# 32-query groups on 64-row array tiles for the attention of three batches out of four, 64-query groups kept for the first

## The chip, the cores and the metric

One core of a Trainium2 chip runs the whole program; everything is fp32. The metric is the device time of one execution in microseconds (us), lower is better. A verdict "faster" or "slower" needs 2%. One execution of the kernel before took 1261.8 us; it lies over 1.5% above the fastest, so it counts as slow and is left out of every ratio.

## The reference

Four batches, eight heads, 768 positions, head width 64. Attention looks at a local window and at 24 block summaries; the result feeds a Fourier mixing layer and a two-layer dense network.

```python
k_sum = k.reshape(B, H, nb, 32, D).max(axis=3)          # 24 blocks of 32
v_sum = v.reshape(B, H, nb, 32, D).mean(axis=3)
scores_l = scale * q @ k.T          where |i - j| < 16, else -1e9
scores_s = scale * q @ k_sum.T + log(32)
x = softmax([scores_l, scores_s]) @ [v, v_sum]          # heads side by side: 768 x 512
u = x + real(fft(fft(x, axis=1), axis=2))
un = (u - mean(u)) / sqrt(var(u) + 1e-6)
out = u + relu(un @ w1) @ w2                            # 512 -> 2048 -> 512
```

## The kernel before: the parts that matter

Heads go in pairs; a batch has four pairs. A *wide* pair is cut into 12 groups of 64 queries, each with a window of 96 keys. The 24 block summaries are rows 96 to 127 of the same score tile, so that one exponential and one mask serve both.

```python
def prepare(b, g):                    # "turning" q and k of a pair, on TensorE
    for src, dst in ((kn, kt), (qn, qt)):
        for j0, j1 in ((0, 2), (2, 3)):
            ps = abank(...)
            # ... 24 matmuls against ident for q and k together, 64-column tiles
            nc.scalar.copy(out=dst[:, 2*P*j0:2*P*j1], in_=ps)      # 4 copies in all, 128 partitions

def scores(b, g):
    for half in range(2):
        for n in range(n0, n1):                                    # 6 groups
            for e in range(2):                                     # 2 heads: two row halves
                nc.tensor.matmul(ps[e][0:96, n - n0, :], kt[rows, 64*n:64*n + 96], qt[rows, 64*n:64*n + 64])
        for e in range(2):
            nc.tensor.matmul(ps[e][96:128], km[rows, :], qt[rows, ...])         # block summaries, 384 columns
        for e in range(2):
            nc.scalar.activation(out=p[:, e, n0:n1], in_=ps[e], func=AF.Exp, scale=SC)
            tt(p[:, e, n0:n1], p[:, e, n0:n1], near[:, n0:n1], ALU.mult)
```

After attention a batch passes through `gen_post`: a Fourier step (`y`), mixing (`mx`: six tiles, each followed on VectorE by the sum with x and the statistics), normalisation and transposes (`unt`), then the dense layers `h` and `o`, which take most of the time.

```python
for t in range(NST):                                  # 6 tiles of 128 positions
    if t % 2: nc.scalar.activation(out=un[:, t, :], in_=x[:, t, :], func=AF.Identity, bias=..., scale=...)
    else:     nc.vector.tensor_scalar(out=un[:, t, :], in0=x[:, t, :], ...)
    for d in range(NDT): nc.tensor.transpose(ps[:, d // 2, d % 2, :], un[:, t, P*d:P*(d+1)], ident)
    (nc.vector.tensor_copy if t % 2 else nc.scalar.copy)(out=u[...], in_=ps)
    yield
```

The attention of batch b + 1 is woven into the post part of batch b, one of its steps after every four of post. Batch 0's attention comes first and alone; batch 1's lies beside batch 0's post part and the conversion of the weights.

```python
for b in range(B):
    attn = gen_attention(b + 1) if b + 1 < B else iter(())
    if b == 0:
        drive((gen_fourier(0), 4, 600), (first(weights, 16), 3, 0), (first(attn, 5), 1, 0))
        drive((gen_channel(0), 4, 0), (weights, 12, 0), (attn, 1, 0))
    else:
        drive((gen_post(b), 4, 0), (attn, 1, 0))
```

I call the time from the first Fourier matmul of batch n to that of batch n + 1 "stage n", and split it at the first mixing matmul (mx), the first transpose of the normalised rows (unt) and the first dense matmul (h).

## Time and profile before

| | us |
|---|---|
| runs before the prediction | 891.82, 892.23 (and the slow 1261.8) |
| stage 0 (batch 1's attention, weight conversion) | 82.2 to 298.8: 216.6 |
| stage 1 (batch 2's attention) | 298.8 to 504.5: 205.7 |
| stage 2 (batch 3's attention) | 504.5 to 707.8: 203.3 |
| stage 3 (no attention) | 707.8 to 881.8: 174.0 |

The windows of the kernel before, cut at the first three of these stages. Columns: window and length, then busy time (with instructions) of PE, PEld, DVE, ACT and POOL, then granted clock, DMA share, GB/s.

```profile
82.20:298.80 216.60, 208.29 (x1209) 152.32 (x1210) 186.03 (x405) 81.74 (x159) 33.45 (x22) 0.99 0.58 183
298.80:504.50 205.70, 205.70 (x1317) 153.45 (x1316) 100.35 (x226) 42.80 (x90) 1.07 (x2) 1.00 0.37 116
504.50:707.80 203.30, 203.30 (x1272) 150.76 (x1270) 100.00 (x229) 41.08 (x86) 0.00 (x0) 1.00 0.30 100
```

TensorE is busy for all of stages 1 and 2.

### The profile page before, as it was taken

The page shows a single profiled execution, that of the slowest core. Times are in us where ns is not written, and L with a number is a line of the kernel's source. Part 1 is how long each engine was busy: PE and PEld are TensorE (multiplying, and loading weights), DVE is VectorE, ACT ScalarE, POOL GpSimd, SP SyncE. Part 2 cuts the span into 40 slices and gives each one's busy share as a digit, 9 for nine tenths or more (in the row PEclk, how much of TensorE's full clock was granted, in tenths as well). Part 3 has the DMA queues.
Part 4 walks back from the last instruction along what each step waited for, and adds up shares of the span by engine and source line. Part 5 has one row for each costly group of instructions (what it writes and reads, how often), then busy time and mean ns, then how long its engine had stood idle before and what let it go on. Part 6 is the DMA issues. An engine that isn't in the chain of part 4 may idle for free.

```text
span 887.9 us, 12940 instructions
## 1 busy us (share of the span) xinstructions
PE 850.9 (96%) x5282; PEld 630.0 (71%) x5282; DVE 505.3 (57%) x1118; ACT 223.5 (25%) x449; POOL 56.0 (6%) x46
## 2 busy tenths in 40 slices
PE   7977999999989999999999999999999988999997
PEld 5755765688558786678758887668757875687586
DVE  1488999976898266353239248254328455442352
ACT  2543365621630224311120034311020022101200
POOL 2404004002050000000000000000000000000000
PEclk9996999999999999999999999999999999999999
DMA  9996776943761463231621372320421171305001
GB/s 207 245 289 169 216 208 215 268 158 110 256 230 42 173 210 105 82 105 36 215 74 60 112 246 60 93 83 1 161 102 59 56 282 44 120 4 189 18 25 50
DMA packets 90020, 119.41 MB, mean 134 GB/s; under 512 B 40448, under 2 KB 73440, under 8 KB 89952
## 3 DMA queue, kind: packets, MB, share of 16 engines
q1 hardware_dynamic: 89408, 117.99, 43.4%
q8 instruction: 43, 0.70, 0.3%
q10 hardware_dynamic: 544, 0.51, 0.2%
q14 instruction: 25, 0.20, 0.1%
HBM read 97.52 MB, written 20.97 MB: 133 GB/s over the span
## 4 chain that ended last, share of the span: by engine, by line
PE 86%; DVE 9%; ACT 2%; DMA 1%; issue 1%; POOL 1%; SPq 0%
PE ox L939 19%; PE hx L892 17%; PE oz L939 9%; PE hz L892 8%; PE sc L606 5%; PE oy L939 4%; PE qk L587 4%; PE hy L892 4%; PE sc L610 3%; PE y L810 3%; PE av L629 3%; PE mx L831 2%; PE mx L833 2%; DVE w L525 2%; DVE fold L525 1%; PE unt L869 1%
## 5 line engine op out<-in xcount | busy, mean ns | idle before, releaser
L892 PE MATMUL hx<-u,w 128*128 128x384 f32 x512 | 184.6, 491 | 4.7 <-ACT h L907 3.1
L892 PEld LDWEIGHTS hx<-u,w 128*128 128x128 f32 x512 | 94.9, 190 | 72.0 <-ACT h L907 5.5
L892 PE MATMUL hz<-u,w 128*128 128x384 f32 x256 | 93.7, 486 | 0.0
L939 PE MATMUL ox<-w,s 128*128 128x256 f32 x384 | 91.8, 382 | 1.7 <-DVE x L525 1.7
L939 PE MATMUL oz<-w,s 128*128 128x256 f32 x384 | 91.6, 379 | 0.0
L939 PE MATMUL ox<-w,h 128*128 128x256 f32 x384 | 89.1, 380 | 0.0
L525 DVE TENSOR_TENSOR x<-ox,x 128x256 f32<-128x256 f32 x96 | 40.5, 423 | 74.4 <-PE ox L939 74.2
L939 PEld LDWEIGHTS ox<-w,s 128*128 128x128 f32 x384 | 71.9, 190 | 14.3 <-DVE x L525 3.0
L939 PEld LDWEIGHTS ox<-w,h 128*128 128x128 f32 x384 | 72.8, 190 | 11.6 <-issue 0.2
L939 PEld LDWEIGHTS oz<-w,s 128*128 128x128 f32 x384 | 72.9, 190 | 10.0 <-issue 0.2
L892 PEld LDWEIGHTS hz<-u,w 128*128 128x128 f32 x256 | 48.6, 190 | 34.0 <-DVE u L525 0.3
L525 DVE TENSOR_TENSOR p<-p,near 128x384 f32<-128x384 f32 x64 | 36.0, 601 | 41.8 <-ACT p L612 41.8
L606 PEld LDWEIGHTS sc<-qt,kt 64*96 64x96 f32 x768 | 41.2, 173 | 20.8 <-issue 12.9
L525 DVE TENSOR_TENSOR h<-hy,h 128x384 f32<-128x384 f32 x32 | 17.8, 556 | 60.5 <-PE hy L892 60.5
L612 ACT ACTIVATE p<-sc 128x384 f32<-128x384 f32 x64 | 28.1, 488 | 88.7 <-PE sc L610 88.7
L606 PE MATMUL sc<-qt,kt 64*96 64x64 f32 x768 | 46.2, 262 | 3.2 <-ACT qt L589 2.7
L892 PE MATMUL hy<-u,w 128*128 128x384 f32 x128 | 46.5, 486 | 0.0
L525 DVE TENSOR_TENSOR h<-hx,h 128x384 f32<-128x384 f32 x32 | 17.8, 556 | 49.5 <-PE hx L892 49.5
L939 PE MATMUL oy<-w,h 128*128 128x256 f32 x192 | 45.6, 380 | 0.0
L816 ACT COPY big<-y 128x192 f32<-128x192 f32 x32 | 10.5, 333 | 133.5 <-PE y L810 133.4
L810 PE MATMUL y<-fs,fold 128*128 128x193 f32 x192 | 37.1, 343 | 6.5 <-DVE fold L795 6.5
L525 DVE TENSOR_TENSOR x<-oz,x 128x256 f32<-128x256 f32 x48 | 20.3, 423 | 36.8 <-PE oz L939 36.8
(92 smaller groups left out, 1111.7 us busy)
## 6 DMA issues: line engine op xcount, KB each, us to landing
w<-dw SPq DMA_DIRECT2D x48, 896.0 KB, 5.1
raw<-in_moe_w_ch_dram SPq DMA_DIRECT2D x32, 512.0 KB, 4.8
dw<-w SPq DMA_DIRECT2D x16, 896.0 KB, 5.9
vw<-in_v_dram SPq DMA_DIRECT2D x30, 288.0 KB, 4.8
kn<-in_k_dram SPq DMA_DIRECT2D x16, 384.0 KB, 4.5
qn<-in_q_dram SPq DMA_DIRECT2D x16, 384.0 KB, 6.0
vb<-in_v_dram SPq DMA_DIRECT2D x16, 384.0 KB, 4.7
out_dram<-x SPq DMA_DIRECT2D x24, 256.0 KB, 2.0
```

Of the source, the lines that this page charges most:

```text
L525: nc.vector.tensor_tensor(out=out, in0=in0, in1=in1, op=op)
L587: nc.tensor.matmul(ps[D * e:D * (e + 1), 2 * P * (j - j0) + s:2 * P * (j - j0 + 1):2], src[:, e, j, D * s:D * (s + 1)], ident, start=True, ...
L606: nc.tensor.matmul(ps[e][0:WK, n - n0, :], kt[rows, QB * n:QB * n + WK], qt[rows, QB * n:QB * (n + 1)], start=True, stop=True)
L610: nc.tensor.matmul(ps[e][WK:P], km[rows, :], qt[rows, QB * n0:QB * n1], start=True, stop=True)
L612: nc.scalar.activation(out=p[:, e, n0:n1], in_=ps[e], func=AF.Exp, scale=SC)
L629: nc.tensor.matmul(av[e][QB * (n % 2):QB * (n % 2 + 1), n // 2, :], p[:, e, n, :], vw[:, e, n, :], start=True, stop=True)
L810: nc.tensor.matmul(y, fgs[par][:, st, P * g:P * (g + 1)], fs[par][:, g % 2, st, :], start=(st == 0), stop=(st == HT - 1))
L816: nc.scalar.copy(out=ty[:, g, par:S2:2], in_=y[:, 0:F2])
L831: nc.tensor.matmul(ps[:, par, :], yt[:, half, 2 * par, cols], fd[:, 3 * par, :], start=True, stop=False)
L833: nc.tensor.matmul(ps[:, par, :], yt[:, half, 2 * par + 1, cols], fd[:, 3 * par + 1 + half, :], start=False, stop=True)
L892: nc.tensor.matmul(ps, w[:, a, kk, :], u[:, r, kk, :], start=start and kk == 0, stop=stop and kk == 1, skip_group_check=True)
L939: nc.tensor.matmul(ps, left[a][:, n, :], wt[2, b, j][:, r, :], start=start and n == 0, stop=stop and n == NC - 1, skip_group_check=True)
```

## The change

The intent: narrow groups of 32 queries need 64-key windows only. The traces give the part of TensorE's array that a matmul uses as rows*columns, 128*128 at the most. The narrow scores use 64*64 tiles, a quarter each, of which four (two heads, two halves of the sequence) are meant to run at once, and the values 64*32 tiles, an eighth each. q and k are turned by 12 full transposes in place of 24 small matmuls. The price: the block summaries no longer ride in the same tiles. They get their own matmuls and exponential (`sum_scores`), a VectorE product (`vs`) and six value matmuls of 130 columns. Batch 0, which runs alone at the start, stays wide.

```diff
+    is_wide = lambda b: b == 0
 def prepare(b, g):
+            if is_wide(b):  # ... as before
+            else:
+                for e in range(2):
+                    ps = abank([P, S2], f"qk_{b}_{g}_{e}")
+                    for j in range(NST // 2):
+                        nc.tensor.transpose(ps[:, P * j:P * (j + 1)], src[:, e, j, :], ident)
                     for s in range(2):
+                        nc.scalar.copy(out=dst[D * e:D * (e + 1), s:S:2], in_=ps[D * s:D * (s + 1)])
+    def scores(b, g):
+        ps = [abank([P, NB2, BLOCK], f"sc_{b}_{g}_{h}") for h in range(2)]
+        for i in range(NB2):                    # 12
+            for h in range(2):                  # half of the sequence
+                for e in range(2):              # head
+                    rows, r = slice(D * e, D * (e + 1)), 64 * (e ^ h)
+                    nc.tensor.matmul(ps[h][r:r + 64, i, :], kt[rows, o:o + 64], qt[rows, o:o + BLOCK], ...)
+        for h in range(2):
+            nc.scalar.activation(out=p[:, h], in_=ps[h], func=AF.Exp, scale=SC)
+            tt(p[:, h], p[:, h], near[:, h], ALU.mult)
+    def sum_scores(b, g, p):                    # 4 matmuls of 384 columns on 4 tiles, one exponential
+    def values(b, g, p, pm, x):
+        nc.tensor.matmul(ps, sel[:, g % 2, :], sums[b, g // 2], start=True, stop=True)
+        tt(vs[:, :, 0:D], ps[...].to_broadcast([P, 2, D]), half_of[...].to_broadcast([P, 2, D]), ALU.mult)
+        # 48 matmuls of 65 columns on 64 x 32 tiles, then 6 of 130 columns with vs as moving operand
 # ... cut: loading of the 64-row value windows, masks and small tables
```

## The prediction

> **What bounds the kernel now.** I read the page first (shares, the 40 slices, the chain), then the windows, to see which engine is full in which stage, then the timeline of TensorE in a steady stage, to price one head pair of the attention.
>
> ```profile
> PE 850.9 (96%) x5282; PEld 630.0 (71%) x5282; DVE 505.3 (57%) x1118; ACT 223.5 (25%) x449; POOL 56.0 (6%) x46
> ...
> PE   7977999999989999999999999999999988999997
> ...
> DVE  1488999976898266353239248254328455442352
> ...
> PE 86%; DVE 9%; ACT 2%; DMA 1%; issue 1%; POOL 1%; SPq 0%
> ```
>
> ```profile
> 90.00:120.00 30.00, 28.56 (x302) 23.82 (x302) 29.44 (x88) 14.94 (x32) 0.00 (x0) 1.00 0.62 184
> ...
> 150.00:180.00 30.00, 28.93 (x206) 18.45 (x206) 29.41 (x65) 17.05 (x35) 0.00 (x0) 1.00 0.89 277
> ...
> 350.00:400.00 50.00, 50.00 (x342) 33.40 (x341) 21.23 (x45) 12.81 (x26) 0.00 (x0) 1.00 0.34 103
> ...
> 600.00:700.00 100.00, 100.00 (x478) 75.59 (x475) 49.81 (x108) 10.87 (x21) 0.00 (x0) 1.00 0.21 77
> ```
>
> The columns of the windows are length, then busy time of PE, PEld, DVE, ACT, POOL, then clock, DMA share and GB/s. TensorE is the bound: 86% of the chain, and 50.0 of 50 and 100.0 of 100 us busy where the attention of batches 2 and 3 is woven into the dense layers of the batch before. There a microsecond of TensorE is a microsecond of the kernel. Batch 1's attention lies between about 54 and 220 us, beside the conversion of the weights: there VectorE is full as well (29.4 of 30), so only what is saved on both counts. Batch 0's own attention (0 to 60 us) stays wide.
>
> The timeline prices a wide pair: start, busy time, engine, line, records. Every fp32 matmul is two records.
>
> ```profile
> 112.91 1.53 PE L869 MATMUL unt<-ident,big 128*128 128x128 f32 x12
> 114.37 1.53 PE L587 MATMUL qk<-ident,kn 128*64 128x128 f32 x24
> ...
> 354.08 1.45 PE L892 MATMUL hz<-u,w 128*128 128x384 f32 x4
> 355.46 1.24 PE L606 MATMUL sc<-qt,kt 64*96 64x64 f32 x24
> 356.63 0.84 PE L610 MATMUL sc<-qt,km 64*32 64x384 f32 x4
> 357.39 1.24 PE L606 MATMUL sc<-qt,kt 64*96 64x64 f32 x24
> ...
> 359.32 1.56 PE L892 MATMUL hx<-u,w 128*128 128x384 f32 x4
> ...
> 367.17 1.45 PE L892 MATMUL hz<-u,w 128*128 128x384 f32 x4
> 368.55 0.41 PE L620 MATMUL vs<-vbs,sel 96*32 96x64 f32 x4
> 368.89 1.53 PE L587 MATMUL qk<-ident,kn 128*64 128x128 f32 x24
> 370.25 1.48 PE L587 MATMUL qk<-ident,qn 128*64 128x128 f32 x24
> 371.66 1.56 PE L892 MATMUL hx<-u,w 128*128 128x384 f32 x4
> ...
> 379.51 1.45 PE L892 MATMUL hz<-u,w 128*128 128x384 f32 x4
> 380.89 1.67 PE L629 MATMUL av<-vw,p 128*64 128x65 f32 x48
> 382.49 1.56 PE L892 MATMUL hx<-u,w 128*128 128x384 f32 x4
> ```
>
> Four h records take 1.29 us (start to start elsewhere in this stage), so I subtract 1.29 from each distance between the h groups around an attention block. Scores: 359.32 - 354.08 - 1.29 = 3.95. Block sums of v and the turning of q and k: 371.66 - 367.17 - 1.29 = 3.20. Values: 382.49 - 379.51 - 1.29 = 1.69. A wide pair costs TensorE **8.84 us**.
>
> [...] the single records of the wide scores start in pairs (the two heads lie in different row halves) 7 ns apart, a pair every 85 ns; the values start in pairs (two column halves) every 58 ns, [...] The trace shows about 0.1 us at each edge (354.08 + 1.29 = 355.37, and the scores begin at 355.46). [...] the narrow one puts both heads into one bank in different partition halves, so no run yet shows whether that costs.
>
> **The change part by part, for one narrow pair on TensorE.**
> - Turning q and k: 24 two-pass matmuls (2.77 of the 3.20 us) become 12 one-record transposes of the same form as the un transposes, 12 in 114.37 - 112.91 = 1.46 us. Estimate 1.5.
> - Scores: 24 matmuls with 96 weight columns become 48 with 64, on four 64x64 tiles (two heads times the two halves of the sequence). 96 passes; if all four tiles run at once, 24 rounds of 58 ns = 1.39, with the edges 1.6.
> - Block-sum scores: still four matmuls of 384 columns, but on four different tiles instead of two and two. Two passes of 384 columns at the 322 ns of an h record = 0.64, edges 0.2: 0.85. With the scores that is 2.45 against 3.95.
> - Block sums of v: one full matmul instead of two small ones, about 0.3 as now (0.34).
> - Values: 24 matmuls become 48 on eight 64x32 tiles, plus 6 of 130 columns for the block sums. 96 passes of 65 columns: 12 rounds of 58 ns = 0.7 if eight run at once, 24 = 1.4 if four. I take 1.0. [...] Edges 0.3. Sum 2.0 against 1.69: this part loses.
>
> Sum 1.5 + 1.6 + 0.85 + 0.3 + 2.0 = 6.25 us, 2.6 less than 8.84.
>
> On the other engines, per pair: VectorE loses two of four masks (601 ns each) and gains one product of 128x128 from PSUM (my estimate 0.25 us, from 423 ns for 128x256): 0.95 us less. ScalarE loses one of four exponentials (488 ns) and the 1433 ns copy of the block sums, and its four turning copies (2 x 588 + 2 x 382 = 1.94 us) become eight of 64x384 at about 478 ns = 3.8: nothing gained or lost, at 25% load. DMA: the v windows go from 96 rows of 12 groups to 64 of 24, a third more bytes (590 to 786 KB a pair, in packets of 256 B); it loads two pairs ahead at a DMA share of 0.2 to 0.6 in these stages, so hidden.
>
> A new wait: the narrow values begin with the v block-sum matmul, then VectorE makes the 128x2x64 operand of the last six matmuls. The instruction order shows it right before the values, behind one or two VectorE operations. The values take about 1.2 us before it is needed; I charge 0.3 us a pair.
>
> What lies on the path: 8 pairs of batches 2 and 3 at 2.6 - 0.3 = 2.3: 18.4 us. Batch 1's 4 pairs: VectorE's 0.95 a pair bounds the gain where it is full, TensorE's 2.3 elsewhere; I take 1.1 x 4 = 4.5. Start: the wide mask is the same load as before under another name, a tiny table more; 0. Total 22.9: 892.2 - 22.9 = 869.
>
> **The rivals.**
> 1. *Only two tiles run at once* [...]. Then the scores take 48 rounds of 58 ns = 2.8 + 0.2, the block-sum scores 4 x 0.32 + 0.2 = 1.5, [...]: with 1.8 for the rest, 9.9 us, one more than wide, and the kernel ends about 8 to 12 us later, near 902. For it: every overlap in this trace is of two. Against: rows and columns overlap each for itself[...]. I give it one in six. A mixture (values four at a time, the sums two) leaves 1.5 us a pair, about 878.
> 2. *TensorE waits for VectorE's new operand*, or for PSUM banks that now need two copies each of 64 rows. Against it: attention has 4 banks, and other work stands between. If each pair stalled 1 us the kernel would land near 877.
> 3. *Gain in batch 1 is swallowed* by VectorE, which sets the pace to 210 us. It costs at most the 4.5 us: 874.
> 4. *Transfers*: more and smaller packets in the first stage, where the DMA share is 0.6 to 0.9 with the weights. Batch 0 stays wide, so only batch 1's loads; at most a few us.
>
> **Range and chances.** Prediction 869. The best case (eight tiles at once, no stall, full gain in batch 1) is 3.0 x 12 = 36, so 857; a mixture or stalls give 877 to 880. Range 860 to 885. 2% is 874.4: the central reckoning lies 5 us below it, so the sum may lose a quarter. Faster 0.64, same 0.28, slower 0.08.
>
> **What would show it.** In the profile after: narrow scores at about 1.6 us for 96 records and the four 384-column matmuls at about 0.75 (right: four tiles at once; 3 and 1.4: rival 1); the first 48 value matmuls at 0.7 to 1.4; transposes at 0.12 us each; TensorE still full from 300 to 700 us, the attention blocks there 2.3 to 2.6 us shorter a pair; waits of the last value matmuls for VectorE under 0.3 us. I am wrong if the narrow blocks are not shorter, or if they are but TensorE idles between 300 and 700 us.

What is cut above are statements about the hardware that no trace of the kernel before showed, and one term of the sum that rested on them: 0.67 us for the six block-sum value matmuls. With it the values came to 1.0 + 0.67 + 0.3 = 2.0 us, the narrow pair to 6.25 and the whole forecast to 22.9 us, or 869. Rival 1's values held the same 0.67 (3.8 us), and are cut too. In the trace of the kernel after, the twelve records of the six start in pairs, 110 to 113 ns from pair to pair (the first two 214), and the next dense matmul follows 0.87 us after their start (382.63 to 383.50). "Passes" are records of the trace, two to an fp32 matmul (24 for the 12 score matmuls at 355.46); a transpose is one (12 for the 12 at 112.91). That a pair of starts is two row halves or two column halves is the author's reading: the records don't name their tile.

## More of the kernel before

The granted TensorE clock in 40 slices, from the page of the kernel before:

```profile
PEclk9996999999999999999999999999999999999999
```

A 9 is 90% or more: one early slice falls below that (the fourth, 67 to 89 us), and none after it.

## The result, and the profile after

| | before | after |
|---|---|---|
| fast runs, us | 890.66 to 892.23 | 883.59 to 884.74 (4 runs) |
| median of all, us | 892.03 | 884.46 |
| ratio | | 0.9919 (0.9899 to 0.9938) |

Ratios here and below are the mean time of one kernel's fast runs over that of the other's fast runs of the same rounds, so not quite the ratio of the medians; the range is a 95% interval. The change won 7.6 us by the medians (7.4 if the slow run of the kernel before is left out), where 22.9 were forecast: within 2%, and just inside the range. The profiled executions differ by 5.4 us (889.66 and 884.22).

From the page of the kernel after:

```profile
PE 829.0 (94%) x6122; PEld 613.4 (70%) x6122; DVE 498.4 (56%) x1107; ACT 229.5 (26%) x473; POOL 49.5 (6%) x48
...
PEclk8978979999999999999999999999999999999999
...
PE 37%; DVE 1%; ACT 0%; issue 0%
```

TensorE's busy time fell by 21.9 us (850.9 to 829.0), close to the whole forecast gain; the time fell by a quarter of that in the same two executions (5.4), by a third by the medians. So the work went away and much of the time stayed. The chain in this page adds up to 38%: it could not be followed back to the start, so its shares can't be set beside the 86% of before.

The first three stages after, by windows with the same columns (stage 3 runs from 701.5 to 876.4, 174.9 us):

```profile
76.30:302.90 226.60, 209.95 (x1489) 153.21 (x1490) 189.59 (x405) 86.92 (x173) 31.44 (x23) 0.95 0.63 183
302.90:502.70 199.80, 196.53 (x1598) 146.49 (x1597) 96.72 (x222) 44.99 (x98) 0.63 (x2) 1.00 0.41 124
502.70:701.50 198.80, 195.53 (x1588) 145.16 (x1586) 96.69 (x225) 40.99 (x90) 0.00 (x0) 1.00 0.33 105
```

Set beside the lines of before, stage 1: TensorE's work fell from 205.7 to 196.5, but the stage only to 199.8, and TensorE stands idle for 3.3 us of it. Stage 2 is the same: 195.5 of work in 198.8. Stage 0 ended 4.1 us later than before (302.9 against 298.8), with a mean clock of 0.95 against 0.99.

The timeline of TensorE for a narrow pair in the steady dense part of stage 1:

```profile
357.62 1.46 PE L1005 MATMUL hz<-u,w 128*128 128x384 f32 x4
359.00 1.60 PE L697 MATMUL sc<-qt,kt 64*64 64x32 f32 x96
360.54 1.56 PE L1005 MATMUL hx<-u,w 128*128 128x384 f32 x4
...
368.38 1.46 PE L1005 MATMUL hz<-u,w 128*128 128x384 f32 x4
369.76 0.85 PE L713 MATMUL ss<-qt,km 64*32 64x384 f32 x8
370.55 0.88 PE L639 MATMUL qk<-ident,kn 128*128 128x128 f32 x6
371.25 0.82 PE L639 MATMUL qk<-ident,qn 128*128 128x128 f32 x6
371.91 1.46 PE L1005 MATMUL hx<-u,w 128*128 128x384 f32 x4
...
379.95 1.45 PE L1005 MATMUL hz<-u,w 128*128 128x384 f32 x4
381.24 0.33 PE L719 MATMUL vs<-vbs,sel 96*128 96x64 f32 x2
381.50 1.20 PE L729 MATMUL av<-vw,p 64*32 64x65 f32 x96
382.63 0.94 PE L734 MATMUL av<-vs,p 64*128 64x130 f32 x12
383.50 1.24 PE L1005 MATMUL hx<-u,w 128*128 128x384 f32 x3
```

By the prediction's own method (distance between the h groups less 1.29): scores 360.54 - 357.62 - 1.29 = 1.63, block-sum scores and turning 371.91 - 368.38 - 1.29 = 2.24, values 383.50 - 379.95 - 1.29 = 2.26. Sum 6.13 us, against 6.25 forecast and 8.84 wide. In an undisturbed block the narrow pair is 2.7 us cheaper, as forecast.

What TensorE waited for in stage 1 after (us in total, times, longest); the same view of the kernel before, over its stage 1, is empty:

```profile
PE unt L982 <- ACT big L975: 1.3, 1, 1.3
PE mx L944 <- ACT big L929: 0.7, 1, 0.7
PE unt L982 <- DVE norm L959: 0.5, 1, 0.5
PE av L729 <- DVE vs L542: 0.4, 1, 0.4
```

All of it lies between mixing and the dense layers (319 to 343 us). The second and third lie in *mx to unt*: 0.7 us for ScalarE's copies of the Fourier result, 0.5 for VectorE's statistics. The largest wait, in *unt to h*, is for ScalarE (ACT), an engine that is 26% busy. Its timeline there, before:

```profile
336.07 0.87 ACT L589 COPY kt<-qk 128x512 f32<-128x512 f32 x2
336.81 0.84 ACT L862 ACTIVATE big<-x,norm 128x512 f32<-128x512 f32 x1
337.53 0.86 ACT L589 COPY qt<-qk 128x512 f32<-128x512 f32 x2
338.26 0.85 ACT L862 ACTIVATE big<-x,norm 128x512 f32<-128x512 f32 x1
```

and after:

```profile
336.80 1.54 ACT L641 COPY kt<-qk 64x384 f32<-64x384 f32 x3
338.37 0.81 ACT L975 ACTIVATE big<-x,norm 128x512 f32<-128x512 f32 x1
339.21 0.51 ACT L641 COPY kt<-qk 64x384 f32<-64x384 f32 x1
339.74 2.05 ACT L641 COPY qt<-qk 64x384 f32<-64x384 f32 x4
341.81 0.58 ACT L983 COPY u<-unt 128x512 f32<-128x512 f32 x1
342.30 0.81 ACT L975 ACTIVATE big<-x,norm 128x512 f32<-128x512 f32 x1
```

The ACTIVATE is a normalisation that TensorE's next transposes need. Before, the two stood 1.45 us apart; after, 3.93, because five half-height copies and one copy of transposed rows lie between them, where before there were two copies.

Stage by stage from the traces, in us:

| | stage 0: y-mx / mx-unt / unt-h / h-end | stage 1 | stage 2 |
|---|---|---|---|
| before | 12.6 / 18.1 / 7.5 / 178.3 | 17.8 / 16.1 / 7.5 / 164.4 | 17.8 / 16.1 / 7.5 / 161.9 |
| after | 12.3 / 19.7 / 13.3 / 181.3 | 14.4 / 16.7 / 9.6 / 159.0 | 14.4 / 16.7 / 9.7 / 158.0 |

Three places answer for the missing gain. *mx to unt* didn't get shorter though a narrow pair's scores lie in it. *unt to h* got 2.1 us longer in stages 1 and 2. And in stage 0 *unt to h* took 13.3 in place of 7.5.

### The profile page after: what moved, and what is told of

It is laid out like the page before. It is cut to its first block, busy times and chain, and to the rows that moved or that the text cites. A ratio compares the mean times of both kernels' runs of the same rounds, so it can differ in the third digit from the quotient of the medians.

```text
span 882.4 us, 14658 instructions
## 1 busy us (share of the span) xinstructions
PE 829.0 (94%) x6122; PEld 613.4 (70%) x6122; DVE 498.4 (56%) x1107; ACT 229.5 (26%) x473; POOL 49.5 (6%) x48
## 5 line engine op out<-in xcount | busy, mean ns | idle before, releaser
L1005 PE MATMUL hz<-u,w 128*128 128x384 f32 x256 | 95.8, 494 | 3.3 <-ACT h L1022 2.3
L542 DVE TENSOR_TENSOR h<-hy,h 128x384 f32<-128x384 f32 x32 | 17.8, 555 | 60.6 <-PE hy L1005 60.6
L542 DVE TENSOR_TENSOR h<-hx,h 128x384 f32<-128x384 f32 x32 | 17.8, 555 | 50.3 <-PE hx L1005 49.3
L1015 ACT COPY h<-hx 128x384 f32<-128x384 f32 x32 | 15.3, 478 | 97.8 <-PE hx L1005 93.5
L1052 PEld LDWEIGHTS oy<-w,h 128*128 128x128 f32 x192 | 36.4, 190 | 5.0
L923 PEld LDWEIGHTS y<-fs,fold 128*128 128x128 f32 x192 | 32.3, 195 | 9.7 <-DVE fold L908 6.8
L1031 ACT ACTIVATE h<-hx 128x384 f32<-128x384 f32 x32 | 15.7, 490 | 86.3 <-PE hx L1005 86.3
```

What stands on the lines that cost most here:

```text
L542: nc.vector.tensor_tensor(out=out, in0=in0, in1=in1, op=op)
L923: nc.tensor.matmul(y, fgs[par][:, st, P * g:P * (g + 1)], fs[par][:, g % 2, st, :], start=(st == 0), stop=(st == HT - 1))
L1005: nc.tensor.matmul(ps, w[:, a, kk, :], u[:, r, kk, :], start=start and kk == 0, stop=stop and kk == 1, skip_group_check=True)
L1015: nc.scalar.copy(out=c11, in_=X)
L1031: nc.scalar.activation(out=c21, in_=X, func=AF.Relu)
L1052: nc.tensor.matmul(ps, left[a][:, n, :], wt[2, b, j][:, r, :], start=start and n == 0, stop=stop and n == NC - 1, skip_group_check=True)
```

## The experiments

The theories, by content (letters in the expectations don't follow the order of this list):

- **Chains of other engines.** TensorE's saving is real, but between mixing and the dense layers other engines set the pace as soon as TensorE is done sooner: VectorE's sums and statistics for mx to unt, ScalarE's copies for unt to h.
- **Rival: the narrow matmuls are dearer than they look**, so the gain was never there.
- **Stage 0: half clock.** Short waits around batch 0's mixing (in the changed kernel 1.78 us at 94.4 and 1.48 at 106.8) bring a spell of half clock (granted clock 0.50 for 13.7 us from 107.4; the kernel before has 1.00 from 85.1 to 180.7); it costs what batch 1's narrow groups save. **Rivals:** VectorE, which is full there with the weight conversion (29.4 of 30 us from 90 to 120 in the kernel before), paces the stage whatever TensorE does; or any added TensorE work would help or hurt by shifting the order.

The first four ran on one chip, beside 7 runs of the kernel before (median 889.17).

**e1: batch 1 wide too.**

```diff
-    is_wide = lambda b: b == 0
+    is_wide = lambda b: b < 2
```

(and one mask buffer for both layouts, loaded again after stage 0.)

> Batches 0 and 1 wide, 2 and 3 narrow. Theory A (stage theory): batch 1's narrow pairs cost time, because they lie where VectorE sets the pace and the shorter TensorE work opens gaps in which the clock falls to half; the changed kernel reaches its first dense stage of batch 1 at 302.9 us against 298.8 before. Then this kernel is faster than the changed one by about 4 us: near 880.5, ratio to before 0.987. Rival B (the gain per pair is simply small everywhere, 7 us over 12 pairs): this kernel has 8 pairs instead of 12 and lands near 887, slower than the changed one.

Measured: 881.6 (879.84 to 882.62), ratio 0.9915 (0.987 to 0.9959). Stage 0: 12.6 / 18.1 / 7.5 / 176.0, no spell of half clock between 89.5 us and the last 3 us; stage 1 as in the changed kernel (199.8). So the gain of the changed kernel comes from batches 2 and 3, and narrow groups in batch 1 bring nothing that shows. That they *cost* the forecast 4 us doesn't show either: the theory wanted a ratio of 0.987, which is the edge of the interval, and the measured one is that of the changed kernel (0.9919).

**e2: narrow only pairs 2 and 3 of batches 2 and 3**, those which lie in the dense layers.

```diff
-    is_wide = lambda b: b == 0
+    is_wide = lambda b, g: b < 2 or g < 2
```

> Narrow only in pairs 2 and 3 of batches 2 and 3 (the pairs that lie in the dense stage, where TensorE is full); all else wide. Theory A: each saves TensorE's full 2.7 us, 4 x 2.7 = 10.8: near 881, ratio 0.988, though only a third of the narrow pairs are left. Rival B (small gain everywhere): 4 x 0.6 = 2.4, near 889.6, ratio 0.997.

Measured: 884.74 (881.38 to 892.19), ratio 0.9937 (0.9882 to 0.9991). The time lies between the two forecasts (0.988 and 0.997) and decides nothing; the stages do. Stage 1: 17.8 / 16.1 / 10.3 / 158.8, stage 2: 17.8 / 16.1 / 10.3 / 156.3. The dense part shrinks by 5.6 us in each stage and has no waits: where nothing but TensorE sets the pace, the saving is had in full, and the rival of dear matmuls falls. Some of the 5.6 is work that only moved, though: 22 more records of values and 58 of the narrow scores now lie in unt to h. Over the whole of stage 1 TensorE's work fell by 4.9 us (205.7 to 200.8), 2.4 a pair. Against that stand 2.2 us of new waits, all in unt to h, where pair 2 is turned: nearly half is given back.

**e3: wide groups, but the narrow turning** (12 transposes and eight copies) in batches 1 to 3. The edit is the change's `prepare` alone, with `if b == 0` in place of `is_wide(b)`.

> The kernel before, wide throughout, with only the turning of q and k in batches 1 to 3 by transposes and eight half-height ScalarE copies. TensorE saves 1.3 us a pair, ScalarE works 2.3 us a pair more. Theory C (in the Fourier stage the ScalarE copies stand ahead of the normalisation and delay it): the four pairs turned in dense stages of batches 2 and 3 gain 5 us in all, the Fourier stages of two batches lose about 2 us each: near 891. Theory D (the Fourier stage is paced by VectorE's chain alone, the copies do not matter): no loss there, near 887.

Measured: 884.29 (882.0 to 884.92), ratio 0.9935 (0.9892 to 0.9979). Stage 1: 16.3 / 17.5 / 10.3 / 159.9. The turning alone makes unt to h 2.8 longer, although it takes 1.3 us of work off TensorE each time: 2.0 us of that are waits, and attention work moved there makes up the rest. Over the stage TensorE's work fell by 4.9 us (205.7 to 200.8), and the stage keeps 1.8 (203.9). The total time alone would have spoken for the other theory: its 887 is a ratio of 0.994, as measured, while 891 (0.9987) lies outside the interval. What in the start and in stage 0 brings the rest is open; the verdict here rests on the waits of stages 1 and 2, and on e4. On TensorE's timeline of this run:

```profile
329.89 0.82 PE L596 MATMUL qk<-ident,kn 128*128 128x128 f32 x6
330.54 1.00 PE L596 MATMUL qk<-ident,qn 128*128 128x128 f32 x6
332.49 0.92 PE L638 MATMUL av<-vw,p 128*64 128x65 f32 x24 [0.95 <-ACT kt L598]
333.87 1.09 PE L878 MATMUL unt<-ident,big 128*128 128x128 f32 x8 [0.46 <-ACT big L871]
```

The turning is over by 331.5, and TensorE then waits for the copies of what it turned, and for a normalisation behind them.

**e4: the same program, with the normalisation step ahead of the attention in order.**

```diff
-            if t % 2:
-                nc.scalar.activation(out=un[:, t, :], ...)
+            with tc.high_priority(200) if b else ExitStack():
+                if t % 2:
+                    nc.scalar.activation(out=un[:, t, :], ...)
 # ... the whole step, transposes and copy included, goes under it
```

> The changed kernel with one thing altered: the normalise-and-transpose steps of batches 1 to 3 are put ahead of attention work in the engines' order, so the last of ScalarE's normalisations comes before five of the copies of turned q and k. No work added or removed. Theory C: each of two Fourier stages gets back 1.5 to 2 us, near 881. Theory D: no change, 884.5.

Measured: 877.69 (873.75 to 880.48), ratio 0.9855 (0.9801 to 0.9909): the lowest and clearly below the kernel before, though within 2% of it. Its interval overlaps slightly with that of the changed kernel (0.9899 to 0.9938), so the step from there is read from the stages. Stage 1: 14.4 / 16.7 / 6.8 / 160.1. No work was removed, only the order changed; the edit moves the step on every engine, and on ScalarE it gives:

```profile
333.81 1.53 ACT L641 COPY kt<-qk 64x384 f32<-64x384 f32 x3
335.37 1.52 ACT L976 ACTIVATE big<-x,norm 128x512 f32<-128x512 f32 x2
```

Both normalisations now stand together behind three copies, and unt to h falls from 9.6 to 6.8. The stage gains 1.8, as 1.1 of that comes back in the dense part, where the attention work now lies. (Part of the 2.8 is such work, too: the waits in unt to h fell from 2.0 to 0.6.) With e5, which removes copies in place of moving them, that settles what held TensorE up in unt to h: the copies in ScalarE's queue.

The next four ran on another chip, beside 11 runs of the kernel before (median 889.04).

**e5: pair 2 turned the wide way**, all else narrow.

```diff
-            if is_wide(b):
+            if is_wide(b, g) or g == 2:
                 for j0, j1 in ((0, 2), (2, 3)):
```

> The changed kernel, but pair 2 of batches 1 to 3, whose q and k are turned inside the normalise-and-transpose step, is turned in the wide way: 24 two-pass matmuls and four full-height ScalarE copies (1.9 us) instead of 12 transposes and eight half-height ones (4.1 us measured). TensorE gets 1.3 us more work per batch, ScalarE 2.2 us less. Theory C: the step from the first transpose to the first dense matmul falls from 9.7 to about 7.5 us in batches 1 and 2, and the whole gets some 3 us faster than the changed kernel although TensorE has more to do. Theory D (ScalarE does not matter): it gets 1.3 us a batch slower.

Measured: 878.52 (875.67 to 882.41), ratio 0.9892 (0.9859 to 0.9925). Stage 1: 14.4 / 16.7 / 7.1 / 160.3. The *dearer* turning on TensorE, 1.3 us more work, makes the stage 1.3 us shorter, because it needs four copies and not eight. The same cause as in e4, from the other side. (The values of that pair also move behind the first dense matmuls in this run, so not all of the 7.1 is due to the copies alone.)

**e6: narrow only pairs 0 and 1 of batches 2 and 3**, the complement of e2.

```diff
-    is_wide = lambda b: b == 0
+    is_wide = lambda b, g: b < 2 or g >= 2
```

> The complement of the run with pairs 2 and 3 only: narrow in pairs 0 and 1 of batches 2 and 3 alone (the pairs in the Fourier and normalisation stage). Theory A: TensorE saves 2.7 us a pair there, but VectorE's chain from the first mixing matmul to the first transpose takes 16.7 us by itself, so only what is saved before it (3.4 us a batch: 17.8 to 14.4) shows, less 0.6: 2 to 3 us a batch, 5 in all, ratio 0.994. If the full gain showed it would be 10.8, ratio 0.988.

Measured: 885.13 (877.33 to 886.44), ratio 0.9949 (0.9913 to 0.9985). Stage 1: 14.4 / 16.7 / 7.1 / 164.5; stage 2: 14.4 / 16.7 / 7.1 / 163.1. y to mx gains 3.4; mx to unt *loses* 0.6, with less TensorE work in it (from the timelines, the attention there took 5.5 us before and 4.3 in this run). The stages gain 3.1 and 1.9; with e2's 2.7 and 2.7 that makes 5.8 and 4.6, and the changed kernel has 5.9 and 4.5. So the parts add up, and nothing is hidden between them.

**e7: the changed kernel again**, to see its spread.

> The changed kernel itself, once more, beside the others on one chip: the time to the first Fourier matmul of batch 1 differs by up to 10 us between executions of kernels that are the same up to there, so the comparison needs it. Expected ratio 0.992, and the stages from there on 199.8 and 198.8 us as in its first profile.

Measured: 883.38 (877.67 to 884.42), ratio 0.9933 (0.9902 to 0.9965). The profiled run has the same spell, 13.7 us at half clock from 106.9, and the same 13.2 in stage 0's unt to h. Five of the six runs lie at 882.4 to 884.4 with mean clocks of 0.969 to 0.975; the sixth, 877.67, had 0.980. So an execution without some of the half clock does occur, and it is some 6 us shorter.

**e8: e1 and e4 together** (batch 1 wide, normalisation first).

> Batches 0 and 1 wide, 2 and 3 narrow, with the normalise-and-transpose steps first: both repairs at once. Theory A with C: the stages of batches 1 and 2 take 198.0 and 197.0 us as in the run with the steps first, batch 0's stage 214 to 216 as with batch 1 wide: 3 to 4 us faster than either repair alone, about 876, ratio 0.983. If batch 1's form does not matter: the same as the steps-first run.

Measured: 878.42 (874.8 to 882.26), ratio 0.9897 (0.9865 to 0.993); stage 0 12.7 / 18.0 / 7.5 / 177.6, stage 1 198.0, stage 2 197.0. Each part does to its stage what it did alone. The sum that was hoped for (0.983) lies outside the interval. It isn't better than e4: keeping batch 1 wide wins back no more than the narrow groups with the order repaired.

The third four, on a third chip, beside 11 runs of before (median 890.91).

**e9 and e10: half of the statistics**, in the changed kernel (e9) and in the kernel before (e10), in stages 1 and 2. Each look is a single run of unknown state, and the statistics are wrong on purpose (over half of each row), though the result stayed within the tolerance. The 0.36 us below is the author's estimate: half the columns of an operation that took 0.69.

```diff
-                nc.vector.bn_stats(out=bst, in_=x[:, t, :])
+                nc.vector.bn_stats(out=bst, in_=x[:, t, 0:HD if b in (1, 2) else DM])
```

> The changed kernel with the row statistics of batches 1 and 2 taken over half of the columns (the result is wrong on purpose): six VectorE operations of 0.69 us become about 0.36, 2 us less in VectorE's chain between the first mixing matmul and the first transpose, nothing changed on TensorE. Theory A: that chain sets the pace there, and the step falls from 16.7 to about 15 us in batches 1 and 2. If TensorE or the copies set the pace: it stays at 16.7.

> The same cut in the kernel before, as the control (wrong on purpose). Theory A: there TensorE itself fills the step (24 mixing matmuls of 0.434, the values of 1.69 and the scores of 3.9 us make 16.0), so it stays at 16.1 us although VectorE has 2 us less to do. If VectorE paced both kernels alike: it falls to about 14.5.

Measured: 881.77 and 887.74. What counts is mx to unt in stages 1 and 2: 16.7 became 15.4 in the changed kernel, and 16.1 stayed 16.1 in the kernel before. So VectorE's chain ends that part only after the change. On TensorE, the changed kernel without the halving:

```profile
331.12 1.60 PE L697 MATMUL sc<-qt,kt 64*64 64x32 f32 x96
332.65 0.83 PE L713 MATMUL ss<-qt,km 64*32 64x384 f32 x2
334.01 1.50 PE L982 MATMUL unt<-ident,big 128*128 128x128 f32 x12 [0.53 <-DVE norm L959]
```

and with it (e9), where the transposes follow the scores at once:

```profile
329.13 1.60 PE L697 MATMUL sc<-qt,kt 64*64 64x32 f32 x96
330.66 1.53 PE L982 MATMUL unt<-ident,big 128*128 128x128 f32 x12
```

The 0.7 us wait for ScalarE's copies at the start of the mixing is in both, and no experiment removed it by itself. VectorE in the changed kernel, without the halving:

```profile
326.05 0.69 DVE L542 TENSOR_TENSOR x<-mx,x 128x512 f32<-128x512 f32 x1 [0.56 <-PE mx L946]
326.77 0.69 DVE L951 BATCH_NORM_STATS2 bst<-x 128x6 f32<-128x512 f32 x1
...
333.33 0.54 DVE L978 TENSOR_SCALAR big<-x,norm 128x512 f32<-128x512 f32 x1
```

From 326.05 on no line shows idle time before it: sum, statistics, sum, statistics, with the small steps of the norm between, until the first normalised tile at 333.33, for which the transposes at 334.01 wait. The halving gained the stage only 0.7 (199.8 to 199.1), since unt to h took 0.6 of it back: there TensorE now waits 1.5 us (before 0.4) for VectorE's operand `vs`, which stands behind the small steps of the next norm, and 1.2 for ScalarE's normalisation. One chain lies behind the other, and shortening one uncovers the next.

**e11: the changed kernel with filler matmuls in batch 0's mixing**, 6 × 0.86 = 5 us of TensorE work that nobody reads (0.86 from start to start in its trace, 89.72 to 90.58).

```diff
+                if b == 0:
+                    busy = bank([P, 512], f"mxbusy_{t}")
+                    nc.tensor.matmul(busy, ident, fd.rearrange("p a n -> p (a n)")[:, 0:512], start=True, stop=True)
                 ps = bank([P, 2, HD], f"mx_{b}_{t}")
```

> The changed kernel with six filler matmuls of 512 columns (0.87 us each at full clock, 5 us in all) among the mixing matmuls of batch 0. They also make the scheduler order the work of this stage anew, so it is a rough test. Theory E (in batch 0's stage the gaps let the clock fall to half for 13.7 us near 107 us, and that is most of the loss there): the half-clock spell near 107 us disappears and the step from first transpose to first dense matmul falls from 13.3 to about 8 us, so that batch 0's stage gets no longer in spite of the filler. If the clock is not the cause: the stage gets about 5 us longer, near 890.

Measured: 880.59 (876.85 to 881.04), ratio 0.9882 (0.9841 to 0.9923): with 5 us *more* work it is some 3 to 4 us shorter than the changed kernel (883.3 to 884.5 in its three sets; the intervals overlap). Stage 0: 12.0 / 22.7 / 8.9 / 178.4, the mixing counted from the first filler. There is no spell of half clock between 79 and 256 us. The first transposes after mixing, in the changed kernel:

```profile
108.29 2.82 PE L982 MATMUL unt<-ident,big 128*128 128x128 f32 x12 [1.48 <-DVE big L978]
```

and in e11:

```profile
110.71 1.53 PE L985 MATMUL unt<-ident,big 128*128 128x128 f32 x12 [1.03 <-DVE big L981]
```

The same twelve matmuls take 2.82 us in the spell and 1.53 without. Not all of stage 0's gain is here, however. Up to the first transposes the filler costs 2.7 us, unt to h then wins 4.4, and another 2.9 come from the dense part, where both runs lose the same to half clock (6.8 us of it in each). That part took 176.0 to 183.5 in the profiled runs, and what moves it is open. The mean clock of 90 to 120 us is 0.79 in the changed kernel and 1.00 in e11:

```profile
90.00:120.00 30.00, 25.84 (x293) 21.55 (x292) 25.05 (x75) 9.89 (x18) 3.37 (x4) 0.79 0.63 171
```

```profile
90.00:120.00 30.00, 25.51 (x317) 19.12 (x316) 29.67 (x85) 13.92 (x26) 3.08 (x4) 1.00 0.71 211
```

**e12: batch 1 wide and the whole Fourier part ahead of the attention in order.** A miss.

```diff
     def gen_post(b):
-        yield from gen_fourier(b)
+        steps, more = gen_fourier(b), True
+        while more:
+            with tc.high_priority(300):
+                more = next(steps, steps) is not steps
+            if more:
+                yield
```

> Candidate for the best: batches 0 and 1 wide, 2 and 3 narrow, and the whole Fourier and normalisation part of batches 1 to 3 put ahead of attention work, so that attention fills its waits. Theory A with C: the stages of batches 1 and 2 fall below the 198.0 and 197.0 us of the run with the normalise steps first, by the 0.7 us wait for the copies of the Fourier result and a part of the 2 us lost to VectorE's chain: 195 to 196 each, ratio 0.982 to 0.985.

Measured: 902.24 (899.89 to 905.37), ratio 1.0131 (1.0099 to 1.0163): 1.3% longer than before, under the 2% but clear of noise. The waits of TensorE show the reason:

```profile
PE ox L1052 <- DVE x L542: 18.8, 3, 9.8
```

The priority pulls VectorE's Fourier work ahead of the sums of the dense layers, for which TensorE then stands. It says nothing on the theories.

After twelve runs it was still open whether the filler helps because it prevents the spell, or for some other reason. The last three ran on a fourth chip, beside 11 runs of before (median 889.11).

**e13: the control: the same filler in the kernel before**, which has no spell near 107 us.

> The kernel before with the same six filler matmuls in batch 0's mixing step. Theory E: in this kernel no half-clock spell fell between 90 and 170 us in any profile, so there is nothing to win and up to 5 us of filler to pay: ratio to before 1.000 to 1.005. Rival F (the filler helps by another order[...], whatever the attention's form): it wins some 4 us here as it did in the changed kernel: 0.995.

Measured: 896.98 (892.41 to 898.86), ratio 1.0098 (1.0069 to 1.0127): the filler costs the kernel before about 8 us, more than the 5 us that were expected at most; the rest is not explained. So it doesn't help by itself. What cost 8 us here cost nothing in the kernel that had a spell to take away. The rival that any filler helps falls; strictly, another shift of the changed kernel's order, without filler, was not tried.

**e14: both repairs in one** (e4's order and e11's filler).

> The changed kernel with the filler in batch 0 and the normalise steps first in batches 1 to 3. If the repairs are independent they add: batches 1 and 2 at 198.0 and 197.0, batch 0's stage near 222 without a spell near 107 us, ratio 0.984 to 0.985, near 876. If the filler won only by chance of the execution: 0.988 to 0.990.

Measured: 877.77 (874.2 to 879.78), ratio 0.987 (0.984 to 0.99). It is no better than e4 alone (0.9855) within the intervals, though stage 0 (222.5, no spell near 107) and stages 1 and 2 (198.0, 197.0) are as wanted. In its profiled run stage 3 took 177.8, not 174 to 175, with 10.2 us of half clock from 718.3; e4's profiled run, also at the slow end of its runs, shows the same. That is one reason seen, not a proof that it is the only one.

**e15: the changed kernel a third time.**

> The changed kernel on the same chip: ratio 0.992 to 0.993, batches 1 and 2 at 199.8 and 198.8 us, a half-clock spell of 13.7 us or two of 3.4 near 100 to 120 us.

Measured: 883.32 (878.79 to 885.07), ratio 0.9928 (0.9895 to 0.9961), with 13.7 us at half clock from 107.5 and 13.2 in unt to h. All three profiled runs of the changed kernel have this spell. Two of these six runs took only 879.6 and 878.8 us, at mean clocks of 0.980 and 0.975; the second is no higher than in the slower runs, so the clock alone doesn't tell the short executions from the long.

## Why the prediction was wrong, point by point

The forecast was a gain of 22.9 us; the profiled pair shows 5.4 and the medians 7.6. On the profiled pair, where every term can be read:

| term | forecast gain | measured | |
|---|---|---|---|
| stages 1 and 2: TensorE work | 20.8 | 16.9 | 205.7 - 196.5 and 203.3 - 195.5 |
| stages 1 and 2: new waits | -2.4 | -6.5 | 3.3 idle in each |
| batch 1 and the start | 4.5 | -4.1 | end of stage 0: 298.8, then 302.9 |
| stage 3 | 0 | -0.9 | 3.4 us of half clock in that execution |
| sum | 22.9 | 5.4 | |

So 17.5 us are missing in this pair: 8.0 in stages 1 and 2, 8.6 in batch 1 and the start, 0.9 in stage 3.

1. **The cost of a narrow pair: right.** 6.13 against 6.25; the score records start in fours, one four every 58 ns (96 records from 359.00 to 360.54), the pace of four tiles at once, so rival 1 falls (it wanted 3 us for the scores; they took 1.63). Both heads write into one bank there, in different partition halves, and at that pace no cost of it shows. The 96 records of values took 1.13 us, between the 0.7 of eight tiles at a time and the 1.4 of four. The wait for VectorE's new operand was over-charged: 0.8 us in the whole run, not 0.3 a pair.

2. **The number of times it lies on the path: slightly wrong.** "8 pairs at 2.6" counts eight turnings. The first pair of a batch is turned one stage earlier, so stage 2 has only three (144 turning records there before, 192 in stage 1): 1.3 us less. And over whole stages a pair saved 2.3 of TensorE work, not 2.6 (9.2 / 4 in stage 1), 2.6 us for eight; that blocks broken into pieces between the mixing and transpose groups cost edges is a guess, not tested by itself.

3. **The failed step: "What lies on the path: 8 pairs of batches 2 and 3 at 2.6 - 0.3 = 2.3".** It took a stage in which TensorE was 100% busy for one in which nothing else could set the pace. In the dense layers that holds: those of stages 1 and 2 show no wait in the profiles of e1 to e11. In the 25 us between mixing and the dense layers it does not. VectorE's sums and statistics end the part from mx to unt (e9, e10), after a 0.7 us wait for ScalarE at its start, and ScalarE's copies hold up unt to h (e3, e4, e5). 6.5 us of waits appeared where 2.4 were allowed. The text had named this as a sign of being wrong: TensorE idles between 300 and 700 us.

4. **"ScalarE: nothing gained or lost, at 25% load": wrong, by an average.** The copies were sized well (3.8 forecast, 4.1 measured: 2.05 for four), and their doubling was seen. It was then dismissed by the load over the whole run. In the trace of the changed kernel the 96 copies of 64x384 take 504 to 507 ns on average, and copies of 128x384 in the dense layers 476 to 478. So halving the height did not shorten a copy, and eight took 4.1 us where four had taken 1.94. And what counted was the queue at one moment, with two normalisations behind eight copies.

5. **Batch 1: forecast +4.5, measured a loss.** Rival 3 had the pace of VectorE there and put the worst case at no gain. It missed the half clock: from 90 to 120 us TensorE was busy for 28.56 us before and 25.84 after, at mean clocks of 1.00 and 0.79. That explains a part. In the traces before and after the spells last 3.4, 6.8, 10.2 and 13.7 us, multiples of one length but for the last of each run, which the end cuts off; what sets the length isn't shown. The changed kernel spends 13.7 us at half clock from 107.4, after waits of at most 1.8 us since 85 (1.78 at 94.4, 1.48 at 106.8), and unt to h takes 13.3 against 7.5; without the spell it takes 8.9 (e11). Filler that removes the spell brings back 3 to 4 us although it is 5 us of work itself (e11), and it costs the kernel before 8 (e13). Over stage 0 the mean clock was 0.99 before, 0.95 after and 0.98 with the filler. The size of the loss is not secured: by the total times batch 1's narrow groups cost about nothing (e1), and 2.9 us of e11's gain lie away from the spell.

**Slips of the text that change nothing.** The best case is 892.2 - 36 = 856, not 857, and rival 1's pair adds up to 10.1, not 9.9 (with the 3.8 for the values that is cut).

**Open.** Not every execution has the long spell: e4 and e9, whose stage 0 has the same order, had two of 3.4 us and 9.1 in unt to h. With batch 1 wide (e1) the spell is gone, but the time is only some 2 us better than the changed kernel's, on other chips, and the ratio the same. What else separates the start of these kernels (the first Fourier matmul comes at 74.8 to 85.9 us, in the kernel before itself at 76.0 in e10 and 82.2 in the first run) is as large as what I would explain, and stays open. What exactly trips the spell, the short waits or the small tiles in that stretch, was not told apart.

## What to carry to other kernels

An engine that is 100% busy in a stage gives back what you take from it only as far as the next-slowest chain there (here 9.2 us less work in stage 1, and 5.9 us less time). Before adding up a saving, find what each other engine must have done by the end of each part of the stage, and how much later TensorE could have been without that showing. Count the *instructions* that a layout puts on a lightly loaded engine, and look at what stands behind them in its queue: here changing the order (e4) took another 1.8 us off each of two stages, where the change had taken 5.9 and 4.5. And where TensorE starts to wait in short steps, look at its clock before looking for more waits: here waits of 1.78 and 1.48 us came before 13.7 us at half clock, in which twelve transposes took 2.82 us and not 1.53.
